# A table of listed tokens in its own tile, two transfers a step, later products, and routing that isn't stopped

## The chip, the core and the metric

The kernel runs on one core of a Trainium2 chip. The metric is the device time of one execution in microseconds. The engines go by these names: PE multiplies matrices, DVE and ACT work on whole tiles (DVE with vector operations, ACT with functions of one operand), POOL here starts the indirect transfers, and SP starts the direct ones.

## What is computed

A gated recurrence over four sequences of 5056 steps and 256 channels, and behind it a layer of eight experts. Each of the 20224 tokens goes to one expert: the logits of all tokens and experts are walked in descending order, and a token is taken if it is free and the expert has room (2528 tokens each).

```python
f = lower_bound + (1 - lower_bound) * sigmoid(f_logit)
h = f[:, t] * h + (1 - f[:, t]) * x[:, t]          # for each t; y[:, t] = h
logits = y.reshape(N, D) @ w_gate                   # N = 20224, D = 256, E = 8
for idx in argsort(-logits.flatten()):              # greedy
    tok, e = divmod(idx, E)
    if assigned[tok] < 0 and counts[e] < N // E:
        assigned[tok] = e; counts[e] += 1
out[mask_e] = relu(y[mask_e] @ w1[e]) @ w2[e]       # w1[e]: 256 x 1024, w2[e]: 1024 x 256
```

## The kernel before

The recurrence and the logits fill the first 160 us. Then `moe` runs the experts, as a list of **328 steps** written out in program order: slots −1 to 7 (slot −1 works ahead on tokens whose expert is known early, slot k on the expert that became full k-th), each slot in chunks of up to four tiles of 128 tokens, each chunk in eight steps for the eight slices of the hidden layer. Slot 0 has steps 32 to 71, slot 1 steps 72 to 111, slot 2 begins at 112. A step (line 1563 and on) is `first`, six products into a tile `pw` (the token rows xh, xl times the first weights in two parts), which ACT and DVE then take over as hh and hl, and `second` of three steps earlier, twelve products py<-w2s,hh and py<-w2s,hl. All of them are recorded with line 100, that of the helper that passes each instruction on; so tiles tell them apart.

Between these products stands the **background work**, as Python generators: `main` finds which expert fills next (`route`, in rounds 0 to 7) and, after round 1, makes the **listing**, `condense` (line 602); `comp[k]` writes the token list of slot k (`compact`, line 539); `sp` splits slot weights into a high and a low part (`split`, line 1210). A generator yields the engine and the tiles that its next piece needs. `Bg.tick` (line 1382) lets it go on if the planner `Pace.due` (line 73) says that those tiles are ready by its own modelled clock. The function `tick` (line 1482) is called between groups of products, decides which generator may go on, and so sets the order of all engines. Each engine then takes its instructions in exactly this order.

**The listing** finds the tokens that are still unassigned after round 1 and packs them into 24 columns (3 and then 21, in eight groups of three). For each group, PE makes three products rt<-RAU,MK into the only buffer of `rt`; DVE makes RD from it, and the compare MK for the next group; ACT runs three Sign passes; DVE makes the token numbers IDD and from them the addresses IDG; and `put` queues three fetches TMP<-hbuf,IDG of the tokens' logits, to be started by POOL. When the eight groups are done, IDD is split into a low and a high part, for a table TB that one product rt<-TB,nsub turns; line 667 writes the low part into IDG. Then the generator waits until four steps after the last fetch (`pending`), and line 681 works on what was fetched, TMP<-TMP,pen.

**Transfers** wait in the list `issues`. At the end of each step `issue` starts one, or two if more than six wait, or three if a fetch of the listing waits, and ties them to the hh of that step (`gate`). `gather` puts the loads of token rows, fl<-hbuf,ids, ahead of the listing's fetches; `load_w` the weights ahead of all. The results go out as out_dram<-y,ids.

`tick` also holds `main` back while slot k + 1's list is being written, if k is at most 1 (line 1486). What is called slot 2 in a kernel that counts from one is slot 1 here.

Of the kernel before, what the change touches and what calls it, by code (L numbers as in the profile page):

```python
# [22 lines left out]
class Pace:  # L23
# [48 lines left out]

    def due(self, eng, tiles, slack):

        now = self.free["PE"]
        at = max(now, self.free[eng])
        return at - now <= slack and all(self.ready.get(self.key(t), 0.0) <= at for t in tiles)

# [28 lines left out]
def kernel(ctx: ExitStack, tc: tile.TileContext, x: bass.AP, f_logit: bass.AP,  # L107
# [9 lines left out]
    P = 128  # L117
# [484 lines left out]
    def condense(rt, put, left):  # L602
# [63 lines left out]
        yield 'DVE',  # L666
        v.tensor_scalar(IDG, IDD, P - 1, None, op0=OP.bitwise_and)
        v.tensor_tensor(IDD, IDD, IDG, op=OP.subtract)
        yield 'DVE',
        v.tensor_scalar(TB[:, 1], IDG, pv, None, op0=OP.subtract)  # L670
        v.tensor_tensor(TB[:, 0], IDD, dcol, op=OP.subtract)
# [451 lines left out]
def moe(ctx, tc, g):  # L1123
# [49 lines left out]

    WAITW, WAITS, SLACK, PAT = 30, 8, 2000.0, 6

# [201 lines left out]
    class Bg:  # L1377
# [4 lines left out]
        def tick(self, force=False, within=None):  # L1382
            if self.done:
                return
            if within is not None:
                self.wait = min(self.wait, int(within))
            if not force:
                if self.wait:
                    self.wait -= 1
                    return  # L1390
                if not pace.due(self.need[0], self.need[1:], SLACK):
                    return
                if self.idle and self.need[0] == "PE" and small[0] != count[0]:

                    self.idle -= 1
                    return
            self.idle = self.patience
            if self.need[0] == "PE":
                small[0] = count[0]
            try:  # L1400
                self.need = next(self.gen)
                self.wait = self.apart
            except StopIteration:
                self.done = True
# [33 lines left out]
    def put(them):  # L1438
        at = max([x + 1 for x, (what, _) in enumerate(issues) if what[0] != "s"], default=0)
        issues[at:at] = [(("d",), f) for f in them]  # L1440

    listing, put_at = [], [0]

# [8 lines left out]

    main = Bg(all_routes())

# [27 lines left out]
    def tick():  # L1482
        nonlocal sp, wn
        count[0] += 1

        if k > 1 or k + 1 not in comp or have(k + 1, "ids", sum(CHUNKS[k + 1][1])):
            main.tick()
# [75 lines left out]
    for i in range(len(todo) + LAG):  # L1563
# [29 lines left out]
        if i >= LAG and (len(behind) > LAG or i >= len(todo)):  # L1593
            second(*behind.pop(0))
        issue((3 if any(what == ("d",) for what, _ in issues) else 2 if len(issues) > 6 else 1) if i < len(todo) else 99, paced=i < len(todo))
        tick()
# [46 lines left out]
```

## Time and profile before

| | us |
|---|---|
| device time, median of 3 runs | 1184.74 |
| lowest and highest run | 1183.57, 1187.41 |
| the profiled execution, device time | 1184.77 |
| its span in the trace | 1183.0 |
| PE busy | 1136.7 (96%) |
| DVE busy | 745.5 (63%) |
| ACT busy | 550.4 (47%) |
| POOL busy | 478.4 (40%) |

The 1.8 us between the profiled execution's time and its span lie outside of what the trace shows. Busy time tells which engine has the least room; an engine's idle time is only worth something where it is the engine that all others wait for. In a row of a timeline, the square brackets give the idle time of the engine before that instruction and what ended it by the trace; "issue" and "remote" stand for a wait whose end the trace doesn't put down to anything.

### The profile page before, as it was taken

The numbers are of one execution on the slowest core, as the hardware profiler recorded it, in microseconds if no ns is written. First come the engines' busy times: TensorE is split into PE (matmuls) and PEld (weight loads), VectorE is DVE, ScalarE is ACT, GpSimd is POOL, SyncE is SP. The second block draws the span as 40 slices with busy tenths as digits, with TensorE's granted clock in tenths as the row PEclk, the third lists the DMA queues.
The fourth block names the chain that finished last, engine by engine and source line by source line (L and its number), as shares of the span: only waits on it lengthen the run. The fifth ranks groups of instructions, "written<-read, shape, count | busy, mean of one in ns | idle before, by whom it ended". The sixth has DMA issues, their size and how long they took to land.

```text
span 1183.0 us, 21830 instructions
## 1 busy us (share of the span) xinstructions
PE 1136.7 (96%) x8180; PEld 1028.6 (87%) x8180; DVE 745.5 (63%) x2203; ACT 550.4 (47%) x1152; POOL 478.4 (40%) x489
## 2 busy tenths in 40 slices
PE   7999989989999889999999999999999999999996
PEld 7999868878888768898889988899888899999996
DVE  6999996667666436677886787667544732352221
ACT  7888763263326533444444453336434622342231
POOL 6777632223333663343433333343334333433321
PEclk9999999999999999999999999999999999999998
DMA  9999993131131011311311311131113111311100
GB/s 341 367 353 374 380 348 109 34 102 42 51 105 48 16 42 54 107 51 51 107 50 42 112 46 45 42 112 50 45 46 102 61 45 46 112 50 46 43 32 27
DMA packets 53215, 125.27 MB, mean 106 GB/s; under 512 B 8832, under 2 KB 29056, under 8 KB 51952
## 3 DMA queue, kind: packets, MB, share of 16 engines
q0 software_dynamic: 20016, 61.02, 16.1%
q1 hardware_dynamic: 32544, 62.78, 15.0%
q8 instruction: 66, 1.08, 0.4%
q14 instruction: 45, 0.37, 0.1%
q10 hardware_dynamic: 544, 0.01, 0.0%
HBM read 81.79 MB, written 42.10 MB: 105 GB/s over the span
## 4 chain that ended last, share of the span: by engine, by line
PE 82%; DVE 4%; DMA 4%; issue 3%; ACT 3%; another core or an unknown queue 1%; POOL 1%; SPq 0%; DVEq 0%; POOLq 0%; ACTq 0%
PE py L100 36%; PE pw L100 34%; PE pr L100 4%; PE rt L100 3%; PE pt L100 2%; DMA r<-in_moe_w_dram,wi 2%; PE pf L100 2%; PE pb L100 2%; DVE g L100 2%; DMA fl<-in_f_logit_dram 1%; ACT hh L100 1%; ACT MK L100 1%; DVE xl L100 1%; DMA hbuf<-hr 1%
## 5 line engine op out<-in xcount | busy, mean ns | idle before, releaser
L100 PE MATMUL py<-w2s,hh 128*128 128x256 f32 x2560 | 493.3, 289 | 3.4 <-ACT y L100 1.9
L100 PEld LDWEIGHTS py<-w2s,hh 128*128 128x128 f32 x2560 | 406.5, 188 | 21.6 <-issue 3.0
L100 ACT ACTIVATE hh<-pw 128x512 fp32r<-128x512 f32 (+3 forms) x328 | 190.7, 582 | 504.0 <-PE pw L100 439.7
L100 DVE SCALAR_TENSOR_TENSOR hl<-pw,hh 128x512 fp32r<-128x512 f32 (+3 forms) x328 | 219.6, 670 | 251.0 <-ACT hh L100 242.7
L100 PE MATMUL py<-w2s,hl 128*128 128x256 f32 (+1 forms) x1280 | 361.6, 283 | 0.0
L100 POOL DMA_INDIRECT out_dram<-y,ids x160 | 162.6, 1016 | 333.0 <-ACT hh L100 256.8
L100 POOL DMA_INDIRECT fl<-hbuf,ids x160 | 162.7, 1017 | 271.6 <-ACT hh L100 211.9
L100 PEld LDWEIGHTS py<-w2s,hl 128*128 128x128 f32 (+1 forms) x1280 | 240.3, 188 | 0.1
L100 PE MATMUL pw<-xh,xl 128*128 128x512 f32 (+3 forms) x672 | 231.7, 387 | 3.0 <-issue 1.4
L100 PEld LDWEIGHTS pw<-xh,xl 128*128 128x128 f32 x672 | 125.2, 189 | 20.0 <-issue 1.8
L100 PE MATMUL pw<-xl 128*128 128x512 f32 (+3 forms) x336 | 129.8, 386 | 1.5 <-DVE xl L100 1.2
L100 PE MATMUL pw<-xh,w1l 128*128 128x512 f32 (+1 forms) x320 | 126.2, 394 | 0.0
L100 PE MATMUL pw<-xl,w1h 128*128 128x512 f32 (+1 forms) x320 | 126.2, 394 | 0.0
L100 PE MATMUL pw<-xh,w1h 128*128 128x512 f32 (+1 forms) x320 | 125.7, 393 | 0.0
L100 POOL TENSOR_TENSOR xl<-fl,xl 128x1024 f32<-128x1024 f32 (+1 forms) x39 | 90.2, 2314 | 37.9 <-ACT fl L100 22.5
L100 DVE TENSOR_TENSOR_SCAN g<-fg,g,pb 128x512 f32<-128x512 f32 (+4 forms) x78 | 92.8, 1227 | 6.3 <-ACT fg L100 4.6
L100 PE MATMUL pr<-iw,g 128*128 128x136 f32 x632 | 81.2, 280 | 2.4 <-ACT hr L100 2.4
L100 PEld LDWEIGHTS pr<-iw,g 128*128 128x128 f32 x632 | 76.5, 190 | 2.9 <-ACT hr L100 2.8
L100 ACT ACTIVATE junk<-rt,r 128x182 bf16<-128x182 f32 (+2 forms) x153 | 61.4, 402 | 31.4 <-DVE r L100 26.9
L100 PEld LDWEIGHTS pw<-xh,w1l 128*128 128x128 f32 x320 | 60.2, 188 | 11.8
L100 PEld LDWEIGHTS pw<-xl 128*128 128x128 f32 x336 | 63.5, 189 | 7.5 <-DVE xl L100 1.5
L100 PEld LDWEIGHTS pw<-xl,w1h 128*128 128x128 f32 x320 | 60.2, 188 | 6.4
(260 smaller groups left out, 1373.5 us busy)
## 6 DMA issues: line engine op xcount, KB each, us to landing
hbuf<-hr SPq DMA_DIRECT2D x39, 528.0 KB
fl<-in_f_logit_dram SPq DMA_DIRECT2D x38, 512.0 KB
xl<-in_x_dram SPq DMA_DIRECT2D x38, 512.0 KB
fl<-hbuf,ids POOLq DMA_INDIRECT x160
out_dram<-y,ids POOLq DMA_INDIRECT x160
fl<-in_f_logit_dram SPq DMA_DIRECT2D x3, 256.0 KB
xl<-in_x_dram SPq DMA_DIRECT2D x3, 256.0 KB
r<-in_moe_w_dram,wi POOLq DMA_INDIRECT x27
```

The costliest lines, as they stand in the source:

```text
L100: r = f(*args, **kw)
```

## The change

Four edits, and one line that moves. (1) The low part of IDD goes to `TR`, a tile that is free at that time, and IDG keeps its addresses. (2) While fetches of the listing wait, two transfers are started in a step, not three. (3) While the listing runs, a background piece for PE is let go only when its tiles have been ready for 700 ns of the planner's clock (`SPARE`); this holds for the token lists too. (4) In slot 0, `main` isn't held back for the list of slot 1. `main` is defined some lines earlier, with no effect by itself.

```diff
--- before.py
+++ after.py
@@ -70,11 +70,11 @@
         for o in outs:
             self.ready[self.key(o)] = end + (2500 if "dma" in op else 220 if eng == "PE" else 70)
 
-    def due(self, eng, tiles, slack):
+    def due(self, eng, tiles, slack, spare=0.0):
 
         now = self.free["PE"]
         at = max(now, self.free[eng])
-        return at - now <= slack and all(self.ready.get(self.key(t), 0.0) <= at for t in tiles)
+        return at - now <= slack and all(self.ready.get(self.key(t), 0.0) + spare <= at for t in tiles)
 
 
 class Paced:
@@ -664,10 +664,11 @@
         v.tensor_tensor(over, tU[:, 0:1], tU[:, 1:2], op=OP.max)
         v.tensor_scalar(out_of, over, 1.0e6, None, op0=OP.mult)
         yield 'DVE',
-        v.tensor_scalar(IDG, IDD, P - 1, None, op0=OP.bitwise_and)
-        v.tensor_tensor(IDD, IDD, IDG, op=OP.subtract)
+        low = TR[:, :ND].bitcast(I32)
+        v.tensor_scalar(low, IDD, P - 1, None, op0=OP.bitwise_and)
+        v.tensor_tensor(IDD, IDD, low, op=OP.subtract)
         yield 'DVE',
-        v.tensor_scalar(TB[:, 1], IDG, pv, None, op0=OP.subtract)
+        v.tensor_scalar(TB[:, 1], low, pv, None, op0=OP.subtract)
         v.tensor_tensor(TB[:, 0], IDD, dcol, op=OP.subtract)
         yield 'PE', TB
         ps = rt.tile([P, 512], F32, name="rt")
@@ -1171,7 +1172,7 @@
     WI, IDS, RAW, WS, XG, XS, HS, PY, SC = {}, {}, {}, {}, {}, {}, {}, {}, []
     WI[-1], IDS[-1], RAW[-1] = g["WIE"], g["IDE"], g["RAWE"]
 
-    WAITW, WAITS, SLACK, PAT = 30, 8, 2000.0, 6
+    WAITW, WAITS, SLACK, PAT, SPARE = 30, 8, 2000.0, 6, 700.0
 
     def loose(k):
         return {} if 0 <= k <= LAST else dict(bounds_check=NT * P - 1, oob_is_err=False)
@@ -1388,7 +1389,7 @@
                 if self.wait:
                     self.wait -= 1
                     return
-                if not pace.due(self.need[0], self.need[1:], SLACK):
+                if not pace.due(self.need[0], self.need[1:], SLACK, SPARE if listing and self.need[0] == "PE" else 0.0):
                     return
                 if self.idle and self.need[0] == "PE" and small[0] != count[0]:
 
@@ -1439,6 +1440,7 @@
         at = max([x + 1 for x, (what, _) in enumerate(issues) if what[0] != "s"], default=0)
         issues[at:at] = [(("d",), f) for f in them]
 
+    main = Bg(all_routes())
     listing, put_at = [], [0]
 
     def pending():
@@ -1450,7 +1452,6 @@
         b, n = CHUNKS[q][min(c + 2 if q == k else 1, len(CHUNKS[q]) - 1)]
         return listing and have(q, "ids", b + n)
 
-    main = Bg(all_routes())
 
     def have(k, what, n=1):
         return k in prog and prog[k].get(what, 0) >= n
@@ -1483,7 +1484,7 @@
         nonlocal sp, wn
         count[0] += 1
 
-        if k > 1 or k + 1 not in comp or have(k + 1, "ids", sum(CHUNKS[k + 1][1])):
+        if k == 0 or k > 1 or k + 1 not in comp or have(k + 1, "ids", sum(CHUNKS[k + 1][1])):
             main.tick()
         flush()
         for q in (k, k + 1, k + 2):
@@ -1592,7 +1593,7 @@
                         trans(*order[nxt], h)
         if i >= LAG and (len(behind) > LAG or i >= len(todo)):
             second(*behind.pop(0))
-        issue((3 if any(what == ("d",) for what, _ in issues) else 2 if len(issues) > 6 else 1) if i < len(todo) else 99, paced=i < len(todo))
+        issue((2 if any(what == ("d",) for what, _ in issues) else 2 if len(issues) > 6 else 1) if i < len(todo) else 99, paced=i < len(todo))
         tick()
     issue(99)
```

The number of instructions on each engine stays the same. The order of 73 steps differs, between steps 56 and about 150. The first product of the listing goes from step 64 to 57, the first of its larger part from 67 to 62, the product with TB from 77 to 75; the search of the next round from 82 to 85, the weights of slot 2 from 93 to 95, the start of slot 2's list from 96 to 99, and the row loads of its first chunk from step 101 to 103, while the transposes of these rows stay at step 107.

On DVE, at the end of the listing, before (the names in square brackets are the queues and engines that an instruction waits for; DMASW are the eight queues of POOL's transfers):

```order
L100 SCALAR_TENSOR_TENSOR hl<-pw,hh 128x512 [waits Activation_49]
L100 TENSOR_TENSOR xl<-pt,xh 128x512 [waits Activation_49]
L100 TENSOR_SCALAR IDG<-IDD 128x24 [waits DMASW4_49,DMASW5_49,DMASW3_49,DMASW6_49,DMASW2_49,DMASW7_49,DMASW1_49,DMASW0_49]
L100 TENSOR_TENSOR IDD<-IDD,IDG 128x24 [waits DVE_49]
L100 TENSOR_SCALAR TB<-IDG,pv 128x24
L100 TENSOR_TENSOR TB<-IDD,dcol 128x24 [waits DVE_49]
L100 SCALAR_TENSOR_TENSOR hl<-pw,hh 128x512 [waits Activation_49]
```

And after:

```order
L100 SCALAR_TENSOR_TENSOR hl<-pw,hh 128x512 [waits Activation_49]
L100 TENSOR_SCALAR TR<-IDD 128x24
L100 TENSOR_TENSOR IDD<-IDD,TR 128x24 [waits DVE_49]
L100 TENSOR_SCALAR TB<-TR,pv 128x24
L100 TENSOR_TENSOR TB<-IDD,dcol 128x24 [waits DVE_49]
L100 SCALAR_TENSOR_TENSOR hl<-pw,hh 128x512 [waits Activation_49]
```

The low part is written to TR and waits for no transfer; the instructions ahead of it are now one hl, without the xl.

On PE, at the sixth of the eight groups of the listing, before:

```order
L100 MATMUL pw<-xh,xl 128x512 x2
L100 MATMUL pw<-xl 128x512
L100 MATMUL pw<-xh,xl 128x512
L100 LDWEIGHTS MK
L100 MATMUL rt<-RAU,MK 128x160
L100 LDWEIGHTS MK
L100 MATMUL rt<-RAU,MK 128x160
L100 LDWEIGHTS MK
L100 MATMUL rt<-RAU,MK 128x160
L100 MATMUL py<-w2s,hh 128x256 x2
```

And after:

```order
L100 MATMUL py<-w2s,hl 128x256
L100 MATMUL py<-w2s,hh 128x256 x2
L100 MATMUL py<-w2s,hl 128x256
L100 MATMUL py<-w2s,hh 128x256 x2
L100 MATMUL py<-w2s,hl 128x256
L100 MATMUL py<-w2s,hh 96x256 x2
L100 MATMUL py<-w2s,hl 96x256
L100 LDWEIGHTS MK
L100 MATMUL rt<-RAU,MK 128x160
L100 LDWEIGHTS MK
L100 MATMUL rt<-RAU,MK 128x160
L100 LDWEIGHTS MK
L100 MATMUL rt<-RAU,MK 128x160
```

The listing's three products have moved from right behind a step's six pw products to behind that step's twelve py products.

On POOL, in the middle of the listing's fetches, before (an instruction that names Activation is the first of its step's transfers, or waits for the hh of that step):

```order
L100 DMA TMP<-hbuf,IDG 128x8 [waits DMASW5_49,DVE_49,Activation_49]
L100 DMA TMP<-hbuf,IDG 128x8 [waits DMASW6_49]
L100 DMA TMP<-hbuf,IDG 128x8 [waits DMASW7_49]
L100 DMA TMP<-hbuf,IDG 128x8 [waits DMASW0_49,DVE_49,Activation_49]
L100 DMA TMP<-hbuf,IDG 128x8 [waits DMASW1_49]
L100 DMA TMP<-hbuf,IDG 128x8 [waits DMASW2_49]
L100 DMA TMP<-hbuf,IDG 128x8 [waits DMASW3_49,DVE_49,Activation_49]
L100 DMA TMP<-hbuf,IDG 128x8 [waits DMASW4_49]
L100 DMA TMP<-hbuf,IDG 128x8 [waits DMASW5_49]
L100 DMA fl<-hbuf,ids 128x264 [waits DMASW6_49,Activation_49]
```

And after:

```order
L100 DMA TMP<-hbuf,IDG 128x8 [waits DMASW3_49,Activation_49]
L100 DMA TMP<-hbuf,IDG 128x8 [waits DMASW4_49]
L100 DMA TMP<-hbuf,IDG 128x8 [waits DMASW5_49,DVE_49,Activation_49]
L100 DMA TMP<-hbuf,IDG 128x8 [waits DMASW6_49]
L100 DMA TMP<-hbuf,IDG 128x8 [waits DMASW7_49,Activation_49]
L100 DMA TMP<-hbuf,IDG 128x8 [waits DMASW0_49,DVE_49]
L100 DMA TMP<-hbuf,IDG 128x8 [waits DMASW1_49,Activation_49]
L100 DMA TMP<-hbuf,IDG 128x8 [waits DMASW2_49]
L100 DMA TMP<-hbuf,IDG 128x8 [waits DMASW3_49,DVE_49,Activation_49]
L100 DMA TMP<-hbuf,IDG 128x8 [waits DMASW4_49]
L100 DMA fl<-hbuf,ids 128x264 [waits DMASW5_49,Activation_49]
L100 DMA fl<-hbuf,ids 128x264 [waits DMASW6_49]
```

Fetches that stood three to a step now stand two to a step, and the next chunk's row loads (fl) stand among them.

## Rows read from the trace of the kernel before

**Rows 1.** The page's busy time, share of the span and instructions of PE and others.
```profile
PE 1136.7 (96%) x8180; PEld 1028.6 (87%) x8180; DVE 745.5 (63%) x2203; ACT 550.4 (47%) x1152; POOL 478.4 (40%) x489
```

**Rows 2.** Four stretches: length, busy PE, PEld, DVE, ACT, POOL (instructions), PEclk, DMA.
```profile
357.50:381.10 23.60, 22.09 (x152) 19.98 (x152) 17.76 (x48) 15.21 (x40) 9.80 (x9) 1.00 0.17 50
...
381.10:397.00 15.90, 15.61 (x114) 14.05 (x112) 8.80 (x31) 9.10 (x28) 8.86 (x9) 1.00 0.14 39
...
397.00:430.00 33.00, 24.44 (x151) 20.55 (x150) 11.53 (x48) 14.35 (x49) 21.37 (x23) 0.95 0.10 18
...
453.00:484.00 31.00, 31.00 (x219) 27.04 (x217) 21.60 (x87) 8.70 (x16) 10.81 (x11) 1.00 0.14 42
```

**Rows 3.** Groups of PE's products, 397 to 430 us: count | busy, mean ns | idle before.
```profile
L100 PE MATMUL py<-w2s,hh 128*128 128x256 f32 (+1 forms) x58 | 11.9, 298 | 1.5 <-issue 1.5
...
L100 PE MATMUL pw<-xh,xl 128*128 128x512 f32 x24 | 9.4, 431 | 1.4 <-issue 1.4
...
L100 PE MATMUL rt<-RAU,MK 128*128 128x160 bf16 x14 | 1.8, 233 | 2.2 <-issue 1.3 <-ACT MK L100 1.0
...
L100 PE MATMUL rt<-TB,nsub 128*128 128x48 bf16 x1 | 0.2, 198 | 3.1 <-ACT hh L100 3.1
```

**Rows 4.** PE's timeline: start, length, instruction, [idle before it <-what ended that].
```profile
359.01 0.30 PE L100 MATMUL rt<-RA,g 128*128 128x160 bf16 x2 [1.81 <-ACT junk L100]
...
404.24 0.37 PE L100 MATMUL rt<-RAU,MK 128*128 128x160 bf16 x3 [1.26 <-issue]
...
427.15 0.20 PE L100 MATMUL rt<-TB,nsub 128*128 128x48 bf16 x1 [3.09 <-ACT hh L100]
```

**Rows 5.** DVE's timeline, the same columns.
```profile
390.64 0.41 DVE L100 TENSOR_SCALAR MK<-IO,STD 128x384 bf16<-128x384 f32 x1
...
424.10 0.69 DVE L100 TENSOR_TENSOR xl<-pt,xh 128x512 fp32r<-128x512 f32 x1 [2.19 <-issue]
...
426.37 0.18 DVE L100 TENSOR_SCALAR IDG<-IDD 128x24 int32<-128x24 int32 x1 [1.58 <-DMA TMP<-hbuf,IDG]
...
440.55 0.36 DVE L100 TENSOR_TENSOR TMP<-TMP,pen 128x192 f32<-128x192 f32 x1
```

**Rows 6.** Chain of waits, 396 to 432 us: shares by line.
```profile
by line: another core or an unknown queue 32.1%; ACT MK L100 18.2%; PE pw L100 10.8%; issue 9.1%; PE py L100 8.9%; ACT hh L100 8.5%; PE rt L100 4.2%; ACT junk L100 3.7%; ACT y L100 2.5%; ACT xh L100 1.7%; PE pt L100 1.3%; ACTq L100 0.2%
```

**Rows 7.** POOL's timeline: the first, the third and the last fetches of the listing.
```profile
388.17 1.01 POOL L100 DMA_INDIRECT TMP<-hbuf,IDG  x1 [0.30 <-ACT xh L100]
...
390.79 1.13 POOL L100 DMA_INDIRECT TMP<-hbuf,IDG  x1 [0.30 <-issue]
...
424.05 1.00 POOL L100 DMA_INDIRECT TMP<-hbuf,IDG  x1 [0.30 <-issue]
...
431.19 1.00 POOL L100 DMA_INDIRECT TMP<-hbuf,IDG  x1 [0.31 <-issue]
```

**Rows 8.** Slices of 4 us: PE busy (instructions), PE's granted clock, DMA.
```profile
408.00:412.00 4.00, 2.92 (x20) 1.00 0.01 0
...
424.00:428.00 4.00, 0.91 (x4) 0.84 0.01 0
...
428.00:432.00 4.00, 4.00 (x23) 0.74 0.16 7
```

**Rows 9.** ACT's timeline: a weight piece, and the last Sign pass of a group.
```profile
356.31 1.28 ACT L100 ACTIVATE xl<-r,omlb 128x512 fp32r<-128x512 f32 x1 [4.99 <-DMA r<-in_moe_w_dram,wi]
...
403.99 0.19 ACT L100 ACTIVATION_READ_ACCUMULATOR MK<-rt,RD 128x1 f32 x1
```

**Rows 10.** Timeline around slot 2's first row loads: ACT, POOL, ACT, PE.
```profile
506.46 0.60 ACT L100 ACTIVATE hh<-pw 128x512 fp32r<-128x512 f32 x1 [0.97 <-PE pw L100]
...
507.33 1.03 POOL L100 DMA_INDIRECT fl<-hbuf,ids  x1 [0.60 <-ACT hh L100]
...
521.10 0.57 ACT L100 ACTIVATE hh<-pw 128x480 fp32r<-128x480 f32 x1 [2.17 <-PE pw L100]
...
523.86 0.46 PE L100 MATMUL pt<-identr,fl 128*128 128x128 f32 x4
```

## The prediction

> **What bounds the kernel now.** I read the page's busy times first: PE, the matrix engine, is busy 96% of the span [rows 1], so only time in which PE stands still, or runs at its lower clock, can be won. Next I read the table of stretches, to find where it stands still [rows 2]. From 453 to 484 us PE is busy 31.00 of 31.00, from 357.5 to 381.1 it is busy 22.09 of 23.60, and in the 33 us from 397 to 430, in which the listing of unassigned tokens runs, only 24.44: 8.56 us of idle PE, at a mean clock of 0.95. The change alters the order of 73 of the 328 steps, all of them around this listing and the list of slot 2, so this stretch, its neighbours and slot 2's first rows are what it can win or lose from.
>
> Third, the groups of PE's products in that stretch tell what the 8.56 us are [rows 3]: 3.1 ahead of the product that reads TB, 2.2 ahead of the listing's products rt<-RAU,MK, and 3.2 in the rest, of which py has 1.5 and pw 1.4. Fourth, the timelines tell what the longest waits for [rows 4, 5]. The trace puts PE's 3.09 at 427.15 down to ACT, but TB is written by DVE, and DVE's way to it is: xl at 424.10, then 1.58 us of waiting for the fetches TMP<-hbuf,IDG, then the write of IDG at 426.37, then three short instructions to TB. IDG holds the addresses of those fetches, so it may not be overwritten while one of them reads it. Fifth, the chain of waits over 396 to 432 us puts 32.1% down to "another core or an unknown queue" [rows 6]: ACT and DVE wait there for products of PE longer than the products' own records explain. I can't name that cause. I note only that POOL issues its fetches back to back in this stretch, 1.00 us each and 0.30 apart [rows 7].
>
> **The change part by part.** The profiled execution took 1184.77 us, the median of the runs is 1184.74, so the sum is made from 1184.77 and needs no correction between them.
>
> *The table in its own tile.* The low part no longer goes to IDG, and in the order DVE's instruction has lost its list of eight queues to wait for. The 1.58 us go [rows 5]. The remaining 1.5 of PE's 3.09 came from xl being late ahead of it; in the new order an hl stands there instead of that xl, so they may go too. Ends 1.6 and 3.1; I take 2.3, the middle, because no row speaks for either end. Behind that idle time the granted clock fell: a slice of 4 us at 0.84 and one at 0.74, that is, part of each at 1.2 instead of 2.4 GHz; the slice from 408 to 412, with 1.08 of idle PE, stayed at 1.00 [rows 8]. The loss is (0.16 + 0.26) × 4 = 1.7 us, of which part lay over idle time. If the clock doesn't fall, most of it comes back, and 0.8 to 1.5 us of idle is nearer to the row of 1.08 than to 3.09: I take 1.3 of 0 to 1.7. Together −3.6 us (ends −1.6 and −4.8).
>
> *Products later, by 700 ns of the planner's time.* PE takes its instructions in order, so a step takes 2.93 us where nothing waits (five lie between the hh at 506.46 and that at 521.10 [rows 10]), and a listing product that is placed before its input is ready stops the expert products behind it. Its input here is the three Sign passes of ACT on the group before, the last of which ends at 403.99 + 0.19 = 404.18; the product starts at 404.24 [rows 4, 9]. At this group, the sixth of eight, the new order puts the step's twelve py products, about half of a step, between pw and the listing's three. Of the 2.2 us [rows 3] the ends are 0 and 2.2; I take 1.8, since 1.4 us would cover the 1.26 here, while other groups stand in front of fewer products. −1.8 us. The same rule now holds for the list of slot 1 while the listing runs, where a product waited 1.81 us at 359.01 for ACT, which had a weight piece of 1.28 us ahead of the needed passes [rows 4, 9]. That is longer than 700 ns, so I take about half: −1.0 us (0 to −1.8).
>
> *Two transfers a step.* POOL's 24 fetches lasted from 388.17 to 431.19, in 12 steps, up to three to a step; three take 3 × 1.30 = 3.9 us [rows 7], more than a step. Two take 2.6 and leave room, and by the order they spread over 19 steps, with 12 row loads between them. POOL itself is off the path. What the pace may give is the 3.2 us in the rest of [rows 3], if they come from POOL's back-to-back work; what it may cost is more steps under transfers. Ends 0 and −3.2 here (the cost is a rival below); I take half, −1.6 us, because I have no row for the cause.
>
> *Routing not stopped, listing earlier.* Round work and listing move ahead into 357.5 to 381.1, where DVE is busy 17.76 of 23.60 already [rows 2]. A crowded DVE delays hl, and PE waits for it. The nearest price is the wait at 359.01, 1.81 us; with 5.84 us of DVE's time free the cost is nearer to nothing: +0.5 us (0 to 1.8).
>
> *Slot 2's first rows.* Its list ends three steps later, and its four row loads are requested at step 103 instead of 101. They go one to a step, each behind the step's hh: the first at 507.33, 0.87 after the hh at 506.46, the fourth three steps later. Two steps later still, the fourth goes 0.87 behind the hh at 521.10, at 521.97 [rows 10]. A fetch takes about 2.3 us from its start to its landing (424.05 to IDG's write at 426.37 [rows 5, 7]), so it lands at 524.3; PE transposes these rows at 523.86 [rows 10]. +0.5 us (0 to 3.0, a step more if a store stands ahead).
>
> Sum: −3.6 − 1.8 − 1.0 − 1.6 + 0.5 + 0.5 = −7.0, so **1177.8 us**. With every gain whole and no cost, −4.8 − 2.2 − 1.8 − 3.2 = −12.0, 1172.8.
>
> **The rivals.** About 0.3%, 3.55 us, is what a measurement of this kernel can tell from no change.
>
> *The waits travel along.* Only the table's part pays; the listing's products find their inputs late wherever they stand. −3.6 + 1.0 = −2.6: 1182.2. For it: the 32.1% of unnamed waiting belongs to ACT and DVE, not to the place of a product [rows 6]. Against: 2.2 of the 8.56 us stand ahead of the listing's own products [rows 3].
>
> *The next wait takes IDG's place.* After the fetches DVE runs TMP<-TMP,pen, which needs all 24 landed. Before, it ran at 440.55, 9.4 us behind the last fetch's start, and a landing takes 2.3 [rows 5, 7], so there are 7 us of room; the order leaves four steps. If the slower pace uses the room up, a wait like the removed one, 3.1 and its clock's 1.7, returns: −7.0 + 4.8 = −2.2, 1182.6. The change then doesn't do what it says.
>
> *More steps under transfers (the slower side).* If PE's waiting is a toll for each step in which POOL fetches, the 2.2 and the 3.2 were 5.4 us in 12 steps, 0.45 a step. Over 19 steps at the same toll it is 8.6, 3.2 more: −2.6 + 3.2 = +0.6, 1185.4. It becomes slower by over 0.3% from (3.55 + 2.6 + 5.4) / 19 = 0.61 a step on; at 0.9 a step, between that and the 1.26 that one step of the rows lost [rows 4], it is −2.6 + 17.1 − 5.4 = +9.1, 1193.9. For it: the waiting is where the fetches are. Against: from 381.1 to 397, where the first fetches run, PE idled 0.29 us [rows 2].
>
> *A fetch held up by VectorE.* A fetch at 390.79, beside a compare on DVE at 390.64 that lasts 0.41, took 1.13 instead of 1.00 [rows 5, 7]: 0.13 more. Were each fetch held for a whole compare, two would take 2 × 1.71 = 3.4 us, 0.5 more than a step, 19 × 0.5 = 9 us by the end of the listing; what is made from the fetches would be late, and the gain gone: about 1185.5. The Trainium skill, "SBUF — State Buffer", section "SBUF: two separate sides", has such a rule: while VectorE runs an operation that takes both of its ports, GpSimd can't write a transfer's descriptors and waits for the operation's end. By that rule the last time would hold; the row shows a hold of a third of the compare at most.
>
> **How the numbers follow.** Likeliest, the sum: 0.64 (0.58 faster, 0.06 within 0.3%; half of its gain takes it to 1181.2, the bound). Waits travel along: 0.12 (0.04 faster, 0.08 same). Next wait: 0.04, same. More steps under transfers: 0.18 (0.06 same, 0.12 slower). VectorE: 0.02, same. Faster 0.58 + 0.04 = 0.62; same 0.06 + 0.08 + 0.04 + 0.06 + 0.02 = 0.26; slower 0.12. The range goes from 1173.0, about where every gain is whole, to 1183.5, which takes in the first two rivals with 0.9 us to spare; left out above it are the third and the fourth, 0.20.
>
> **What would show it.** In the changed profile the write of TR should show no wait for fetches, the product with TB should wait under 1 us, and no slice behind it should fall below 0.95. The listing's products should wait under 0.5 us in sum; idle PE from the first fetch to the last should be under 4 us. Fetches should come in pairs with POOL idle between them. The transposes of slot 2's first rows should wait under 1 us. I would be wrong if the unnamed waits stand there as before although POOL has pauses, if TMP<-TMP,pen waits for fetches, or if waiting appears before 381 us in place of what left the listing.

## The result, and the profile after

| | before | after |
|---|---|---|
| median, us | 1184.81 (5 runs) | 1173.18 (5 runs) |
| lowest and highest, us | 1183.57, 1187.41 | 1170.77, 1173.80 |
| profiled execution, us | 1184.77 | 1172.39 |
| its span, us | 1183.0 | 1170.6 |

The ratio is 0.9888, with a 95% interval of 0.9875 to 0.9902: **13.3 us faster** by the ratio (1184.81 × 0.0112), 12.4 by the two profiled executions, 11.6 by the medians. The forecast was 1177.8 and a range from 1173.0 to 1183.5; the ratio gives 1171.5 (its interval 1170.0 to 1173.2), so the sign and the place were right and the gain was nearly twice the one forecast.

Where it came from is read from the tables of stretches. Columns here are the stretch, its length, PE's busy time (instructions), its granted clock, the DMA share and GB/s. Of the kernel before:

```profile
330.00:385.00 55.00, 51.93 (x382) 1.00 0.24 80
385.00:440.00 55.00, 46.15 (x301) 0.97 0.12 29
440.00:520.00 80.00, 78.07 (x533) 1.00 0.23 71
520.00:1000.00 480.00, 480.00 (x3272) 1.00 0.20 62
```

and of the changed kernel:

```profile
330.00:385.00 55.00, 54.50 (x400) 1.00 0.25 80
385.00:440.00 55.00, 54.87 (x375) 1.00 0.15 36
440.00:520.00 80.00, 77.53 (x529) 1.00 0.22 74
520.00:1000.00 480.00, 479.85 (x3270) 1.00 0.20 62
```

From 330 to 520 us PE idled 3.07 + 8.85 + 1.93 = 13.85 us before and 0.50 + 0.13 + 2.47 = 3.10 after, and the clock's 0.03 × 55 = 1.65 us came back (a small part of it lay over idle time): 10.75 + 1.65 = 12.4, about the whole difference of the spans. The listing, which had 8.56 us of idle PE [rows 2], has 0.13.

What the forecast asked to look for: the write of TR waits for nothing, and TB follows at once (DVE's timeline of the changed kernel, where [rows 5] had 1.58 us of waiting):

```profile
407.55 0.17 DVE L100 TENSOR_SCALAR TR<-IDD 128x24 int32<-128x24 int32 x1
407.75 0.18 DVE L100 TENSOR_TENSOR IDD<-IDD,TR 128x24 int32<-128x24 int32 x1
407.85 0.27 DVE L100 TENSOR_SCALAR TB<-TR,pv 128x24 bf16<-128x24 int32 x1
```

No product of the listing waits, and no slice falls below 1.00 there. Another sign failed: fetches were to come in pairs with POOL idle between them, and they do so only up to 400 us. Behind that POOL runs four, six and eight transfers 0.30 us apart. The last of these stretches, POOL's timeline of the changed kernel:

```profile
416.69 0.99 POOL L100 DMA_INDIRECT TMP<-hbuf,IDG  x1 [2.17 <-ACT hh L100]
...
425.80 1.00 POOL L100 DMA_INDIRECT TMP<-hbuf,IDG  x1 [0.30 <-issue]
```

And unnamed waits there still are. PE's and ACT's timelines of the changed kernel:

```profile
412.68 0.39 PE L100 MATMUL pw<-xh,xl 128*128 128x512 f32 x1
415.83 1.09 ACT L100 ACTIVATE hh<-pw 128x512 fp32r<-128x512 f32 x2 [4.80 <-remote]
```

The last product of the step ended at 413.07, and ACT, idle for 4.80 us, took it up at 415.83, 2.8 us late. PE went on without a pause: `second` uses hh three steps later, and no product of the listing stood behind ACT at that moment. What was lost anew is small: PE's timeline of the changed kernel, behind the listing and at slot 2's first rows:

```profile
440.94 0.35 PE L100 MATMUL pt<-identr,fl 128*128 128x128 f32 x2 [0.49 <-issue]
442.96 0.27 PE L100 MATMUL rt<-CR,tot 128*128 128x8 f32 x1 [1.24 <-DVE CR L100]
...
511.21 0.28 PE L100 MATMUL pt<-identr,fl 128*128 128x128 f32 x1 [0.58 <-DMA fl<-hbuf,ids]
```

The waits at 440.94 and 442.96 stand beside another late result: ACT took hh at 441.02, 4.16 us after the step's last product had ended at 436.86. The trace names this wait "PE pw", so counting the unnamed waits alone misses some.

### The profile page after: what moved, and what is told of

The parts are those of the page before. It is cut to its first block, busy times and chain, and to the rows that moved or that the text cites. A ratio compares the mean times of both kernels' runs of the same rounds, so it can differ in the third digit from the quotient of the medians.

```text
span 1170.6 us, 21818 instructions
## 1 busy us (share of the span) xinstructions
PE 1135.6 (97%) x8180; PEld 1026.6 (88%) x8180; DVE 744.7 (64%) x2203; ACT 550.1 (47%) x1152; POOL 478.3 (41%) x489
## 4 chain that ended last, share of the span: by engine, by line
PE 86%; DVE 4%; issue 3%; DMA 3%; ACT 1%; POOL 1%; SPq 0%; another core or an unknown queue 0%; POOLq 0%; DVEq 0%; ACTq 0%
PE py L100 37%; PE pw L100 35%; PE pr L100 4%; PE rt L100 3%; PE pb L100 2%; PE pf L100 2%; PE pt L100 2%; DMA fl<-in_f_logit_dram 1%; DVE g L100 1%; DMA r<-in_moe_w_dram,wi 1%; DVE xl L100 1%; POOL fl L100 1%; DMA fl<-hbuf,ids 0%; ACT fg L100 0%; POOL out_dram L100 0%
```

## The experiments

The runs of one group below share one chip, and groups met different chips. That turned out to matter: the kernel before took 1184.8 to 1185.7 us on some (the measured result, groups 1 and 4) and 1173.4 to 1174.6 on the others (groups 2, 3 and 5). I call them **chips with late results** and **quiet chips**, for a reason that group 2 shows. Each chip was met in one group only, so what belongs to the chip and what to the occasion isn't told apart; the names stand for both. Ratios are to the kernel before on the same chip; a difference from the change is taken from its ratio in the first line of the table, measured in another group.

| kernel | chips with late results | quiet chips |
|---|---|---|
| the change | 0.9888 (0.9875 to 0.9902) | 0.9912 (0.9889 to 0.9936) |
| the table's edit alone | 0.9991, 0.9989 | 0.9921 (0.9908 to 0.9935) |
| the change without the table's edit | 0.9908, 0.9916 | 0.9907 (0.9894 to 0.9920) |
| the change without the 700 ns | 0.9957, 0.9931 | |
| the change with three transfers a step | 0.9989 (0.9976 to 1.0002) | 0.9916 (0.9895 to 0.9937) |
| two transfers a step alone | | 0.9980 (0.9970 to 0.9990) |
| the change without the fourth edit | | 1.0018 (1.0006 to 1.0029) |

The 700 ns were taken out on chips with late results alone, the fourth edit on a quiet chip alone; what each is worth on the other kind isn't shown.

### Group 1: parts alone, parts undone

**The table's edit alone** (the second hunk of the diff, on the kernel before). 

> The kernel before with the first edit alone: the low part goes to TR, IDG stays. PE's order is the same as before. If the table's wait is what its rows showed, PE's 3.09 us ahead of rt<-TB shrinks by 1.6 to 3.1 us, and the clock's 1.7 us may come back: 1180.0 to 1183.2, faster by 1.6 to 4.8 us. The waits ahead of rt<-RAU,MK (2.2 us) and the unnamed ones of ACT (over 9 us in sum) stay. If the unnamed waits came from the wait for the fetches, they go with it, and the time is under 1179.

Ratio 0.9991 (0.9979 to 1.0003), 1.1 us, less than the 1.6 to 4.8 expected. PE's timeline shows the edit doing what it should, and the gain given back (its first two lines answer to the 1.81 and the 3.09 of [rows 4]):

```profile
357.53 0.30 PE L100 MATMUL rt<-RA,g 128*128 128x160 bf16 x2 [0.35 <-ACT junk L100]
424.15 0.20 PE L100 MATMUL rt<-TB,nsub 128*128 128x48 bf16 x1 [1.50 <-DVE IDD L100]
439.22 0.37 PE L100 MATMUL rt<-RA,g 128*128 128x160 bf16 x3 [0.68 <-ACT junk L100]
442.99 0.23 PE L100 MATMUL rt<-RA,g 128*128 128x160 bf16 x1 [1.01 <-ACT junk L100]
449.79 0.16 PE L100 MATMUL rt<-FL,eighth 128*128 128x1 bf16 x1 [1.18 <-DVE FL L100]
```

3.09 became 1.50, 1.59 less, the 1.58 of DVE's wait to a hundredth. But 0.68, 1.01 and 1.18 stand behind it that weren't there, and the other waits of the listing (1.28, 0.99, 1.58, 1.05 and so on) stayed, as did the clock's loss (0.97 over 385 to 440 us). The first line tells something else: PE's order is that of the kernel before, and yet the 1.81 us are 0.35, so most of that wait belonged to one execution.

**The change without the table's edit.** 

> The changed kernel without its first edit: the low part overwrites IDG again, everything else as changed, PE's order the same. When the low part is written only 14 of the 24 fetches have been queued (20 of 24 in the kernel before), so the remaining ten fetch other rows than meant; the amount of work is the same. The write must wait for the fourteenth fetch, which in the changed kernel starts at 412.20 and would land near 414.5, while TB is made at 407.9. If DVE's wait is passed on to PE, PE idles some 6 to 7 us ahead of rt<-TB and loses 1 to 2 us of clock: 1178.5 to 1182, so the table part is worth more in the new order than the 3.6 us forecast. If the table part is worth what the order of before showed, 1174 to 1177.

Ratio 0.9908 (0.9887 to 0.9929): 2.4 us behind the change, with intervals that overlap. DVE's timeline of this kernel:

```profile
409.59 0.17 DVE L100 TENSOR_SCALAR IDG<-IDD 128x24 int32<-128x24 int32 x1
```

The overwriting write waits for nothing at all, though it must wait for 14 fetches: with two a step they had all landed. My expectation had the fourteenth start at 412.20 in the changed kernel; it starts at 404.30, 3.25 us before TR's write at 407.55, and 412.20 is the fifteenth. That was a miscount of mine.

**Without the 700 ns.**

```diff
-    WAITW, WAITS, SLACK, PAT, SPARE = 30, 8, 2000.0, 6, 700.0
+    WAITW, WAITS, SLACK, PAT, SPARE = 30, 8, 2000.0, 6, 0.0
```

> The changed kernel with the 700 ns set to 0, two transfers a step and all else as changed. If later products are what took the waits away (placement), the listing's products wait for ACT again, 2 to 5 us in sum, 1174 to 1177. If the pace of two transfers took them away, PE stays full through the listing and the time is 1171 to 1173.

Ratio 0.9957 (0.9941 to 0.9973), so 8.2 us slower than the change, more than either theory allowed. One listing product waits for ACT, and the clock falls behind it. PE's timeline, then slices of 4 us (busy PE, clock):

```profile
393.80 0.37 PE L100 MATMUL rt<-RAU,MK 128*128 128x160 bf16 x3 [2.31 <-ACT MK L100]
```

```profile
392.00:396.00 4.00, 2.20 (x11) 0.84 0.02 4
396.00:400.00 4.00, 4.00 (x25) 0.74 0.07 3
```

2.31 us of idle and (0.16 + 0.26) × 4 = 1.7 of clock; 0.85, 0.78 and 1.41 stand in later stretches, with about 1.6 of clock more (0.98 over the 80 us from 440 to 520). The 2.31 go back to a late result, too. The group before, on PE, and the DVE instruction that takes it up:

```profile
387.98 0.38 PE L100 MATMUL rt<-RAU,MK 128*128 128x160 bf16 x3
391.89 0.16 DVE L100 TENSOR_TENSOR RD<-sq,rt 128x3 f32<-128x3 f32 x1 [4.40 <-PE pw L100]
```

The products ended at 388.36, DVE began 3.53 us later, and the Sign passes and the next group follow from there. So here the later place of a product covers results that come late.

**Three transfers a step.**

```diff
-        issue((2 if any(what == ("d",) for what, _ in issues) else 2 if len(issues) > 6 else 1) ...
+        issue((3 if any(what == ("d",) for what, _ in issues) else 2 if len(issues) > 6 else 1) ...
```

> The changed kernel with up to three transfers a step again. If POOL's back-to-back fetches made the unnamed waits and these stopped PE (pace), 2 to 5 us of idle PE come back around the listing: 1174 to 1177. If the place of the products decides, PE stays full: 1170.5 to 1173. Either way ACT should show unnamed waits of 2 to 5 us.

Ratio 0.9989 (0.9976 to 1.0002): this one number takes back 12 of the 13.3 us, far more than the 2 to 5 expected. The planner sees other ready times with it, so PE's order differs from the change's as well. PE, then ACT, then slices of 4 us, of this kernel:

```profile
399.19 0.38 PE L100 MATMUL rt<-RAU,MK 128*128 128x160 bf16 x3 [3.28 <-ACT MK L100]
```

```profile
414.04 0.60 ACT L100 ACTIVATE hh<-pw 128x512 fp32r<-128x512 f32 x1 [6.71 <-remote]
```

```profile
396.00:400.00 4.00, 0.81 (x5) 0.93 0.10 7
400.00:404.00 4.00, 4.00 (x20) 0.65 0.02 1
428.00:432.00 4.00, 1.71 (x7) 0.77 0.10 33
432.00:436.00 4.00, 4.00 (x14) 0.50 0.13 51
```

The unnamed waits are longer than in any other kernel (6.71, another of 8.00 and one of 5.91), PE is stopped, and the clock falls to its lower level of 1.2 GHz for a whole slice. So on this chip the pace, with the order that comes with it, decides. Why POOL's pace should make PE's results late was the next question.

### Group 2: another chip, and a surprise

**Two transfers a step alone** (the `issue` line of the diff, on the kernel before). 

> The kernel before with the second edit alone: two of the listing's transfers a step instead of three. If the pace is what stopped PE, the unnamed waits shrink and with them most of the 8.56 us of idle PE and the clock's loss: 1174 to 1179. If the pace pays only together with the later products, the listing's products still wait for ACT and the write of IDG for its fetches: 1181 to 1187. The planner sees other ready times, so PE's order moves too.

**The change without the fourth edit** (`k == 0 or` taken out). 

> The changed kernel without the fourth edit: in slot 0 routing stops for the list of slot 1 again. If this edit only moves work between stretches that have room, the time stays within 2 us of the changed kernel's: 1170 to 1175. If the listing's earlier start is what gives the fetches and the lists their room, the waits come back: 1176 to 1184.

Here the kernel before took 1173.4 us, as little as the change had on the first chip, and none of the four traces of this group has a single unnamed wait. Two a step alone had a ratio of 0.9980; it fills the listing (54.23 of 55 us busy) but loses at slot 2's first rows. PE's timeline and slices of two_only:

```profile
504.55 0.28 PE L100 MATMUL pt<-identr,fl 128*128 128x128 f32 x1 [2.29 <-DMA fl<-hbuf,ids]
505.93 0.50 PE L100 MATMUL pt<-identr,fl 128*128 128x128 f32 x2 [1.10 <-DMA fl<-hbuf,ids]
```

```profile
504.00:508.00 4.00, 2.35 (x11) 0.61 0.23 71
508.00:512.00 4.00, 4.00 (x17) 0.53 0.00 0
```

3.4 us of idle and, of (0.39 + 0.47) × 4 = 3.4 of clock, 2.9 over busy time: 6.3 of the 8.0 us that separate it from the change as group 3 measured it. Without the fourth edit the ratio is 1.0018, 12.4 us behind the change: the listing is full there too (55.00 of 55), but slot 2's list is late, one of its products waits 2.95 us and the rows 0.73 and 0.98, and the clock is 0.96 over the 80 us from 440 to 520. So the second edit makes slot 2's rows late, and the fourth is what brings them back in time; neither is about the listing's products.

**Bursts.** In the changed kernel 36 extra fetches into a tile of their own, meant for four places in slots 4 to 6.

```diff
+        if i in (204, 228, 252, 276):
+            for c_ in range(9):
+                nc.nc.gpsimd.indirect_dma_start(out=XB[:, c_], in_=lg, in_offset=off(IDG[:, c_:c_ + 1]), ...)
```

> The changed kernel with four bursts of nine extra fetches, of the listing's kind into a tile of their own, started by POOL back to back behind steps 204, 228, 252 and 276, where PE was full and no listing runs. If POOL's back-to-back transfers make PE's results reach ACT and DVE late, each burst of about 11.7 us shows unnamed waits of ACT or DVE of 2 to 5 us, without any work of the listing around; PE has three steps to spare for hh and stays full, so the time grows by 0 to 3 us. If the unnamed waits belong to the listing's own chain of products and Sign passes, the bursts show none over 0.5 us.

This missed its aim: nothing tied the fetches to a step, and POOL's order, which is not written out by hand, put them into the listing. It tells another thing: 36 × 1.30 = 47 us more on POOL brought the ratio to 1.0229, 27 us above the kernel before and some 37 above the change as group 3 measured it, since row loads queued behind them landed late. PE's timeline:

```profile
441.37 0.37 PE L100 MATMUL pt<-identr,fl 128*128 128x128 f32 x1 [10.34 <-DMA fl<-hbuf,ids]
```

All of it is named, no wait is unnamed, although POOL ran 85 transfers in a row, 0.30 us apart.

**One extra fetch a step** (each tied to its step's hh). 

> The same 36 extra fetches, but one behind each of nine steps, each tied to that step's hh, beside the transfer that the step has anyway. If back-to-back work is the cause, no unnamed wait over 0.5 us, and the time of the changed kernel within 1.5 us. If the number of transfers and not their closeness is the cause, unnamed waits as in the bursts.

Ratio 0.9954 (0.9938 to 0.9969), no unnamed wait, PE 479.92 of 480 us busy from 520 to 1000. That is some 5 us above the change as group 3 measured it on another quiet chip, where 1.5 were expected, while the profiled executions' spans are 1164.6 and 1165.8; its trace shows no place behind the listing where PE waits for it, so I leave this difference open.

### Group 3: the two kernels on a quiet chip

> The changed kernel itself, to have its ratio beside runs of the same chip. In the last group of runs the kernel before took 1173.4 us, 12 less than in the first, and no trace of that group has an unnamed wait. If the unnamed waits depend on the chip, then on a chip without them the change gains 0.4 to 0.8%, and on one with them 1.1%; if the gain is the change's own, 1.1% on either.

> The kernel before itself, for its trace on this chip. If the unnamed waits depend on the chip: none where the kernel before takes near 1173 us, with PE's idle time from 397 to 430 us near 5 instead of 8.56 us; on a chip where it takes near 1185, the same waits at the same places as in the first trace. If they come from the order of the instructions, the same waits on any chip. The time is that of the kernel before, ratio 1.

The change: 0.9912 (0.9889 to 0.9936), 10.3 us: 0.88%, between the 0.4 to 0.8% and the 1.1% expected, with an interval that takes in both, so this run doesn't decide between them; the kernel before against itself 0.9994 (0.9978 to 1.0009). No unnamed wait in either. But PE's idle time in the kernel before, from 397 to 430 us, is 6.47 where I had expected near 5, and it stands in one place. DVE's timeline, PE's timeline, and slices of 4 us, of the kernel before on this chip (beside [rows 5], [rows 4] and [rows 8]):

```profile
415.10 0.18 DVE L100 TENSOR_SCALAR IDG<-IDD 128x24 int32<-128x24 int32 x1 [7.92 <-DMA TMP<-hbuf,IDG]
```

```profile
415.88 0.20 PE L100 MATMUL rt<-TB,nsub 128*128 128x48 bf16 x1 [6.47 <-DVE TB L100]
```

```profile
412.00:416.00 4.00, 0.12 (x2) 0.74 0.01 0
416.00:420.00 4.00, 4.00 (x17) 0.50 0.11 2
420.00:424.00 4.00, 4.00 (x26) 0.91 0.19 35
```

DVE waits 7.92 us for the twentieth fetch (POOL started it at 412.78), PE 6.47. The clock's fall comes to (0.26 + 0.50 + 0.09) × 4 = 3.4 us, but the first slice's 1.0 lies over the idle time, so 2.4 are added: 8.9 us, most of the change's gain on this chip. POOL's chain from the fourth to the twentieth fetch is nearly as long on both kinds of chips (26.2 us here, 29.0 on the first chip). I read this so: with late results PE loses part of that time earlier, in pieces, and only 3.09 are left for this place.

**Three a step again.** 

> The changed kernel with up to three of the listing's transfers a step, as before, beside the changed kernel on the same chip. If three a step cost 12 us only through unnamed waits and the clock that falls behind them, then on a chip without unnamed waits it costs under 3 us against the changed kernel; if POOL's crowding itself costs the time, 8 to 13 us on any chip.

Ratio 0.9916, 0.5 us from the change. The same kernel, with the same order on every engine, that cost 12 us in group 1 costs nothing that can be measured where no result is late, although POOL runs 38 transfers 0.30 us apart in it.

**The bursts, held back to their steps** (each fetch tied to hh). 

> The 36 extra fetches again, now each group of nine held back to steps 204, 228, 252 and 276, where PE is full; in the run named burst POOL had taken them up early, in the middle of the listing. Back to back they last 11.7 us a group and hold up the row loads behind them. If back-to-back transfers make PE's results late, unnamed waits of 2 to 5 us stand in each group, on a chip that shows them at all; else none over 0.5 us. PE stays full, or waits up to 3 us a group for row loads: 0 to 12 us over the changed kernel.

Ratio 0.9943 (0.9923 to 0.9963), 3.6 us above the change with intervals that overlap. In the trace the bursts cost nothing: PE is busy 265.00 of 265.00 us from 800 to 1065 us, and no wait is unnamed.

### Group 4: again a chip with late results

> The kernel before with the table's edit alone, as in tab_only, there 1.1 us faster on a chip with unnamed waits. Where there are none, the trace of the kernel before shows 6.47 us of idle PE ahead of rt<-TB, all from DVE's wait for the twentieth fetch, and the clock falling to half behind it: 3.4 us more. If this wait is the whole of what the change wins there, the edit alone wins 7 to 10 us, nearly as much as the whole change: ratio 0.991 to 0.994. If the waits return elsewhere, as they did in tab_only, 0 to 3 us. On a chip with unnamed waits, 0 to 2 us.

> The changed kernel without the table's edit, as in no_tab: ten of the 24 fetches read overwritten addresses and fetch other rows; the work is the same. In no_tab DVE's write of IDG waited for no fetch, since with two transfers a step only 14 are queued ahead of it and these had landed. So the pace replaces the table's edit: within 2 us of the changed kernel, ratio 0.989 to 0.993. If the listing runs ahead of the fetches where nothing disturbs it, DVE waits for the fourteenth and PE idles 3 to 6 us: ratio 0.994 to 0.998.

> The changed kernel with the 700 ns set to 0, as in no_spare, there 8 us slower than the changed kernel on a chip with unnamed waits, with 2.31 us of idle ahead of one listing product and the clock falling behind it. If later products serve only to cover results that come late, then without unnamed waits it is within 2 us of the changed kernel, ratio 0.989 to 0.993; if they cover ACT's ordinary Sign passes, 0.994 to 0.998.

Here the kernel before took 1184.9 us, and unnamed waits were back. The table's edit alone 0.9989 (0.9975 to 1.0004), the change without it 0.9916 (0.9900 to 0.9931), without the 700 ns 0.9931 (0.9916 to 0.9947): as in group 1, the last one a little better. The change itself wasn't run in this group.

**The held bursts on this chip.** 

> The 36 extra fetches at four places of full PE, as in burst_late, which showed no unnamed wait on a chip without them. If this chip is one with unnamed waits: 2 to 5 us of them in each group if back-to-back transfers make PE's results late, none over 0.5 us if only the listing does. If it is one without, as in burst_late: none, PE full, and 0 to 4 us over the changed kernel.

This is the experiment that tells. The same instructions in the same order as burst_late, and on PE, DVE and ACT the order of the change: ratio 1.0094 (1.0069 to 1.0120, from two runs), 21 us above the change without the table's edit in this group, and a span of 1191.1 us, 20.5 longer than the change's. One row of a window, 800 to 1065 us, of burst_late_again (PE busy, clock), and what ACT and DVE waited for from 520 on in it (total us, times, longest):

```profile
800.00:1065.00 265.00, 255.24 (x1637) 0.98 0.20 59
```

```profile
ACT hh L100 <- remote: 14.5, 5, 6.6
DVE r L100 <- remote: 5.9, 1, 5.9
ACT y L100 <- remote: 0.8, 1, 0.8
```

and of burst_late on the quiet chip, the same window:

```profile
800.00:1065.00 265.00, 265.00 (x1752) 1.00 0.20 62
```

Step by step against burst_late, the four bursts cost 3.2, 6.9, 5.1 and 2.4 us, 17.6 in sum, and the steps between them nothing. In this stretch no listing runs, and where the changed kernel has no bursts PE is busy 479.85 of 480 on a chip of this kind. The unnamed waits come to 7.1, 5.9, 6.6 and 1.7 us in the four groups, where 2 to 5 were expected. So here transfers that POOL starts back to back make PE's results late without any listing around; on a quiet chip they don't.

The bursts add transfers as well as crowding them, and spaced ones were added on a quiet chip alone. The traces kept tell the two apart. An hh is ready when the last of its six products and ACT's instruction before it have ended; it is counted as late if it starts over 0.6 us after that. All 328 hh of the ten traces of each kind, by whether POOL was then in a row of four or more transfers 0.30 us apart:

| hh became ready | late, chips with late results | late, quiet chips |
|---|---|---|
| within such a row | 51 of 150 | 0 of 198 |
| outside | 7 of 3130 | 0 of 3082 |

The 58 are 0.67 to 8.0 us late, and the 51 start within the row or at most 2.0 us behind its end; on quiet chips no hh is over 0.10 us late. So it is the closeness of the transfers, and on these chips alone. A late hh also holds POOL back and so makes the next row longer; the bursts, which were placed by hand, show which comes first.

### Group 5: the table's edit on a quiet chip

> The kernel before with the table's edit alone, once more, since both runs so far met chips with unnamed waits. On a chip without them: 7 to 10 us faster than the kernel before, ratio 0.991 to 0.994, if the 6.47 us of idle PE and the 3.4 us of clock behind it are the whole of what the change wins there; 0 to 3 us if waits return elsewhere. On a chip with unnamed waits 0 to 2 us, as twice before.

> The changed kernel without the table's edit, once more (ten fetches read overwritten addresses; the work is the same). On a chip without unnamed waits the listing runs ahead of the fetches: if the fourteenth fetch has landed when IDG is overwritten, ratio 0.989 to 0.993, like the changed kernel; if not, PE idles 3 to 6 us ahead of rt<-TB and the ratio is 0.994 to 0.998. On a chip with unnamed waits 0.989 to 0.993, as twice before.

The table's edit alone: 0.9921 (0.9908 to 0.9935). The change without it: 0.9907 (0.9894 to 0.9920). In both PE is busy 55.00 of 55 us from 385 to 440. DVE's timelines, of the one and of the other:

```profile
408.49 0.19 DVE L100 TENSOR_SCALAR TR<-IDD 128x24 int32<-128x24 int32 x1
```

```profile
401.13 0.18 DVE L100 TENSOR_SCALAR IDG<-IDD 128x24 int32<-128x24 int32 x1 [0.26 <-issue]
```

On a quiet chip, then, either way wins the whole: give the low part a tile of its own, or have, by the other three edits, only 14 fetches, already landed, ahead of the write instead of 20. They don't add up.

## Why the prediction missed, point by point

- **The place** was right: nothing behind 520 us moved, and the listing gave the gain.
- **Two transfers a step**, −1.6 of a possible −3.2, "I take half, because I have no row for the cause": this is the step that failed: the size of this term, and that it was added to the others as if they were apart from it. All 3.2 went, and three a step took 12 us back on the same kind of chip, where the term had 1.6; on a quiet chip they took back 0.5, within noise. I had put the bound of this term at the waits with no other owner; but the pace also decided the waits that I had booked under the table and under later products (2.2 and 3.09), since ACT's Sign passes and xl were late for the same reason (the 17.6 us of the held bursts show crowded transfers doing this by themselves). A cause that stands in the chain with 32.1% [rows 6] should have been priced across all the waits that it touches, and not in a term of its own.
- **The table**, −3.6: in the changed kernel the 3.09 and the clock's 1.7 are gone whole, 4.8, the end of my range (by the trace 1.5 of the 1.7 lay over busy time). But the edit isn't what did it there: alone it won 1.1 us, with 1.59 less at TB, as the 1.58 of [rows 5] said, 2.9 of new waits behind, and the clock's fall still there. I was right on the row and wrong on what is late next. On a quiet chip, where this wait was 6.47 us, the edit alone won 9.3.
- **Later products**, −1.8 of 2.2: all of it went. Without the 700 ns the change loses 8.2 us in one group and about 5 in the other ((0.9931 − 0.9888) × 1185), so undoing the edit costs over twice the term: I counted the idle time and not the clock that falls behind it, 1.7 us a time, nor waits in other stretches. The parts undone one at a time (12, 8.2 and 2.4 us) come to more than the whole, so they can't be read as shares of it.
- **The list of slot 1**, −1.0 of 1.81: all went, though most of it wasn't the edit's to win: with the order of before, group 1's table edit had 0.35 there, and the changed kernel on a quiet chip has 1.60 at a product of the same kind (356.93). With it went 0.92, 0.55 and 1.39 in other stretches, for which I had no term at all, because I read the listing's stretch closely and the others by their sums only. PE's timeline of the kernel before:

```profile
351.92 0.23 PE L100 MATMUL rt<-RS,nsub 128*128 128x160 bf16 x1 [0.92 <-DVE RS L100]
...
452.08 0.26 PE L100 MATMUL rt<-O,MK 128*128 128x64 bf16 x3 [0.55 <-DVE MK L100]
...
500.32 0.50 PE L100 MATMUL py<-w2s,hh 128*128 128x256 f32 x2 [1.39 <-ACT y L100]
```

- **The costs**, +0.5 for a crowded slot 0 and +0.5 for slot 2's rows: 0 and 0.58. Not foreseen: 1.24 at rt<-CR,tot and 0.65 at transposes behind the listing, both beside the hh that was 4.16 us late.
- **The rivals.** Waits that travel along: they do without the 700 ns (2.31 ahead of a listing product), not with it. The next wait at TMP<-TMP,pen: it ran at 431.92 right behind an hl, with no wait. More steps under transfers: the opposite; a toll there is, but by closeness, not by the number of steps, and on chips with late results alone. A fetch held up by VectorE: the 24 fetches took 991, 997 and 1077 ns (least, median, most), so none was held by more than 0.09 us (its 1185.5 didn't come out of the rows either). The rule of the Trainium skill ("SBUF — State Buffer", "SBUF: two separate sides") doesn't show in these transfers; whether VectorE's work beside them was of the kind that it names isn't known.
- **The range** ended at 1173.0, where every gain is whole. It left out that gains could come from waits outside of the listing (2.9 us). New waits took back most of these: the profiled executions differ by 12.4 us, against 12.0 with every gain whole, and the step from there to the ratio's 13.3 lies within its interval. That the time fell below the range and not just into it may be noise. That all gains came out whole together follows, as I read it, from the one cause that I had priced apart.

## What to carry to other kernels

Before a wait is priced, ask what the instruction ahead of it waited for: if several waits of a stretch go back to one cause, price the cause over all of them, and add the clock's loss to a wait where the trace shows one. A tile that serves as the addresses of transfers is in use until they have landed: give later results a tile of their own, or see that the transfers ahead are few and done. And where a burst of transfers isn't urgent, spread it: three a step instead of two cost 12 us of 1185 on one chip and 0.5, within noise, on another. Look then at what queues behind it: by itself the slower pace made slot 2's rows 3.4 us late.

## What the runs showed of the hardware

Chips, or occasions, differ in a way that makes the order of instructions matter. In the first result and on two more of the chips met, transfers started by POOL back to back made results of PE reach ACT and DVE up to 8.0 us late, in every kernel run there and in a stretch without the listing; on three others no result was late, with rows of up to 85 such transfers, and the kernel before took 1173.4 to 1174.6 instead of 1184.8 to 1185.7 us. What makes the results late, and whether it hangs on the transfers' small pieces or on POOL's work alone, stays open: no run here tells.

The recording itself is a rival that no run rules out. Of the landing records of transfers (16 to each, 7920 or, with extra fetches, 8496 in all) the ten traces with late results lack 1163 to 1865, the ten quiet ones 11 to 29, and most are lacking where POOL's transfers are crowded: from 350 to 450 us the changed kernel has 396 on the first chip and 919 on a quiet one. Every run on record was traced, so none tells whether results would be late in an execution that isn't.

The clock's fall comes on top of a wait: behind 2.31 us of idle PE it cost 1.7 us of busy time, behind 6.47 us 2.4.
